# Decode attention beside an MLP on one core: the order of work behind the last K block, who copies the last P blocks, and matmuls per loop round

## The chip, the cores and the metric

One core of a Trainium2 chip. The metric is the device time of one execution in microseconds (us), the median of several runs. The engines are TensorE (PE; PEld is its weight load), VectorE (DVE), ScalarE (ACT) and GpSimd (POOL); SyncE (SP) issues nearly all transfers (DMA).

## What is computed

```python
W = min(4096, max(256, Sk // 4))                  # 2048 of the 8192 cached positions
q = (x @ wq).reshape(B, Sq, Hq, Dh)               # B=8, Sq=1, Hq=32, Dh=128, D=576
k = repeat(k_cache[:, :, Sk - W:, :], 2, axis=1)  # 16 heads of K and V, each for two heads of q
v = repeat(v_cache[:, :, Sk - W:, :], 2, axis=1)
p = softmax(einsum("bhqd,bhkd->bhqk", q, k) * Dh ** -0.5)
a = einsum("bhqk,bhkd->bhqd", p, v).reshape(B, Sq, Hq * Dh) @ wo
y = layernorm(x)
b = gelu(y @ w1 + b1) @ w2 + b2                   # F=4608
g = sigmoid((x * gate_w).sum(-1, keepdims=True))
return g * a + (1 - g) * b
```

All tensors are bf16. The window of K and of V is 67 MB each, against some 20 MB of weights; each byte is read once.

## The kernel before

The core reads 16 blocks of K and 16 of V, 4 MB each. Four groups (of 32 pairs of batch and K head) are each cut into four blocks of 512 positions, so block n belongs to group n // 4. Transfers are issued by SP in one order: wq, w1, K0, K1, V0, K2, V1, K3 and so on to K15, V14, V15, then b2, 24 rows of w2 in two pieces, wo in four pieces, and the last 12 rows of w2 in pieces of 8, 3 and 1 (here a row is one of the 36 rows that a partition holds). Four slots of on-chip memory take them in turn; the issue of a block waits until its slot is free. The slot of K15 takes the first three pieces of wo; the slot of V14 takes the fourth piece and the last three of w2.

For K block n (`k_unit`): VectorE makes four 32x32-block transposes (L693, `tr`), each into one of two halves of the tile `KT`; after each, TensorE adds one score unit (L711 and, through the helper that keeps the weights, L175), two groups of four matmuls of 512 columns. A transpose waits until the score unit of two transposes earlier has read its half. When all four units are done, `softmax` takes the maximum on VectorE (L644, `mx`), scales it (L646/L648, `nb`), and ScalarE makes the exponential P (L650); ScalarE then writes the mask for the next block's scores (L654).

For V block n (`v_item`): VectorE transposes P by 32x32 blocks (L668, `pt`, made in `spread`). Four block copies (L742 on ScalarE, L743 on GpSimd or VectorE) lay the result out as a block-diagonal operand; which engine takes each of the four is in `px_engs`. Then 64 matmuls multiply it with V (`pv`): two at the head, a hardware loop of rounds whose matmuls take their addresses from registers (L186, `BODY` of them in a round), two at the tail (L752). The last block, n = 15, has no loop: 48 and 16 matmuls (L752), its operand is laid out in the area of `KT`, which GpSimd first sets to zero (L726) when K15's scores are done. VectorE then adds the result to the running output (L788/L790, `o`). At a group's end come small sums across partitions (L674 to L681, with two tiny matmuls), a weighting on VectorE (L793, L796) and GpSimd (L798), and the matmul `us` (L801).

At the end, ScalarE and VectorE evict and transpose the attention output (L804, L805), and TensorE accumulates the product with wo (four blocks `proj0` to `proj3`, 16 matmuls each) and that with w2 (`m2`), all on L580, into one accumulator. Its order on TensorE: bias and the first 12 rows of w2 (28 matmuls), `us`, then 24 of the second 12 rows, 64 of the four blocks and 16 of the 8-row piece (104 together), four fillers into the score area, whose result nobody reads (`keep_warm`, L815 and L175), and 8 for the pieces of 3 and 1 rows. Two engines evict the accumulator (L885, L886) and two transfers write the output (L888).

The order on each engine is found when the program is built: a planner takes, of the operations that are ready, the one with the earliest start by the costs written beside them; `deps` are real waits, `after` only fixes an order of starts. So the costs decide the order, and nothing else at run time.

Of the kernel before, what the change touches and what calls it, by code (L numbers as in the profile page):

```python
# [38 lines left out]
class _Plan:  # L39
# [10 lines left out]
    def add(self, eng, fn, deps=(), name=None, cost=0.1, after=(), prio=0):  # L50
        op = _Op(eng, fn, deps, name, cost, after=after, prio=prio)
        op.idx = len(self.all)
        self.all.append(op)
        return op
# [138 lines left out]
def build_kernel(nc, A_x, A_k_cache, A_v_cache, A_wq, A_wo, B_x, B_w1, B_b1, B_w2, B_b2, gate_w, out):  # L193
# [10 lines left out]
    NL = 4 * NG  # L204
# [17 lines left out]
    with ExitStack() as es:  # L222
# [100 lines left out]
        maskq, maskv, swp, pair = view("maskq"), view("maskv"), view("swp"), view("pair")  # L323
# [45 lines left out]
        def col(i, parts=128):  # L369
# [3 lines left out]
        ps = es.enter_context(nc.psum_tensor("ps", [128, 8, 512], F32))  # L373
# [4 lines left out]
        BK_S = 6  # L378
# [8 lines left out]
        add, dma = P.add, P.dma  # L387
# [7 lines left out]
                   deps=[o_idf], name="r8", cost=0.2)  # L395
# [30 lines left out]
        for s in range(2):  # L426
            o_xz.append(add("dve", (lambda s=s: lambda e: e.tensor_copy(xz[:, s, :].rearrange("p (k z) -> p k z", z=2)[:, :, s], x_sb[:, 512:576]))(),  # L427
                            deps=dx + [o_xz0], name="xz%d" % s, cost=0.12))
# [12 lines left out]
        for s in range(2):  # L441
            o_yz.append(add("dve", (lambda s=s: lambda e: e.tensor_copy(yz[:, s, :].rearrange("p (k z) -> p k z", z=2)[:, :, s], y_bf[:, 512:576]))(),
                            deps=[o_y, o_yz0], name="yz%d" % s, cost=0.12))
# [35 lines left out]
        o_swp = []  # L479
# [108 lines left out]
        for vi in range(NL):  # L588
            stream.append(("V", vi))
            if vi + 2 < NL:  # L590
                stream.append(("K", vi + 2))
        HEAD, BODY, TAIL = 2, 20, 2
        ROUNDS = (64 - HEAD - TAIL) // BODY
        assert HEAD and TAIL and HEAD + ROUNDS * BODY + TAIL == 64
        held_regs = []
# [16 lines left out]
        grp_done, acc_done = {}, {}  # L612
        mask_done, mx_done = {}, {}
        grp_first, sums = {}, {}
        px_engs = [("pool", "pool", "act", "act")] * (NL - 1) + [("pool", "act", "act", "dve")]

        def take_slot():
            n = n_slot[0]
# [44 lines left out]
        def spread(n, after=()):  # L663
            g, i = divmod(n, 4)
            k = lambda m, j: sm[:, m, j:j + 1]
            MX, NB, S, AL, SS = range(5)
            ex, nb = ex_done[n], nb_done[n]
            pt_done[n] = add("dve", lambda e: e.transpose(bass.AP(arena, offset=aoffs("PT") + 2048 * (n % 2), ap=[[AST, 128], [1, 2048]]), Pm),  # L668
                             deps=[ex] + (px_done[n - 2] if n >= 2 else [o_yTp, o_hT]), name="pt%d" % n, cost=2.3, prio=5, after=after)
            if i == 3:  # L670
                G = lambda j: sg[:, g, j:j + 1]
                NBQ, WT, SW, RC, CF = range(5)
                prev = grp_done.get(g - 1, [])
                sw_pe = add("pe", lambda e: e.matmul(ps[:, BK_S, 4:5], swp, k(n, NB), start=True, stop=True), deps=[nb, o_u] + o_swp + prev, name="sw_pe%d" % g, cost=0.5, prio=3)  # L674
                nbq = add("dve", lambda e: e.tensor_tensor(out=G(NBQ), in0=k(n, NB), in1=ps[:, BK_S, 4:5], op=ALU.min), deps=[sw_pe], name="nbq%d" % g, cost=0.16, prio=3)
                grp_first[n] = nbq
                wt = add("act", lambda e: e.activation(out=G(WT), in_=k(n, NB), func=ACTF.Exp, bias=G(NBQ), scale=-1.0), deps=[nbq], name="wt%d" % g, cost=0.25, prio=3)
                sw = add("dve", lambda e: e.tensor_tensor(out=G(SW), in0=k(n, SS), in1=G(WT), op=ALU.mult), deps=[wt, ss_done[n]], name="sw%d" % g, cost=0.16, prio=3)
                su = add("pe", lambda e: e.matmul(ps[:, BK_S, 0:1], pair, G(SW), start=True, stop=True), deps=[sw, o_pair] + prev, name="sum_pe%d" % g, cost=0.5, prio=3)  # L679
                rc = add("dve", lambda e: e.reciprocal(out=G(RC), in_=ps[:, BK_S, 0:1]), deps=[su], name="rc%d" % g, cost=0.16, prio=3)  # L680
                cf = add("dve", lambda e: e.tensor_tensor(out=G(CF), in0=G(WT), in1=G(RC), op=ALU.mult), deps=[rc], name="cf%d" % g, cost=0.16, prio=3)  # L681
                grp_done[g] = [nbq, rc, cf]
                sums[g] = su

        def k_unit(n, s, d):
            g, i = divmod(n, 4)
            trs = []
            for rh in range(2):
                for hh in range(2):
                    m = 4 * n + 2 * rh + hh  # L690
                    kb = m % 2
                    deps = [d] + ([qk_half[m - 2]] if m >= 2 else [o_selp])
                    tr = add("dve", (lambda rh=rh, hh=hh, kb=kb: lambda e: e.transpose(bass.AP(arena_f, offset=foffs("KT") + kb * 2048, ap=[[AST // 2, 128], [1, 2048]]),  # L693
                                                                                      bass.AP(arena_f, offset=foffs("RAW") + s * SE + rh * (SE // 2) + 32 * hh, ap=[[AST // 2, 128], [64, 64], [1, 32]])))(),
                             deps=deps, name="tr%d_%d%d" % (n, rh, hh), cost=2.3, after=tr_hist[-1:] + ([mx_done.get(n - 1)] if rh + hh == 0 else []) + ([pt_done.get(n - 1)] if rh == 1 else []))
                    tr_hist.append(tr)
                    trs.append(tr)
                    if n and rh == 0 and hh == 1:
                        spread(n - 1, after=[tr])
                    if rh == 1 and hh == 0:  # L700
                        for op in (o_done.get(n - 2), grp_first.pop(n - 1, None)):
                            if op is not None:
                                op.after.append(tr)

                    def qk_fn(e, rh=rh, hh=hh, kb=kb):
                        mm = None
                        for ee in range(2):
                            for rc in range(4):
                                rhs = bass.AP(arena, offset=aoffs("KT") + kb * 4096 + rc * 1024 + ee, ap=[[AST, 128], [2, 512]])
                                args = (ps[:, rc, :], qbd[:, g % 2, 2 * hh + ee, rh, :], rhs)  # L710
                                mm = e.matmul(*args, start=False, stop=True, skip_group_check=True) if rc == 0 else held_matmul(nc, e, *args, stop=True, skip=True)  # L711
                        return mm
                    deps = [tr]
                    if rh == 0 and hh == 0:
                        deps += qb_done[g] + [mask_done[n]]
                    qk = add("pe", qk_fn, deps=deps, name="qk%d_%d%d" % (n, rh, hh), cost=1.85, after=qk_half[-1:] + pv_hist[-1:])
                    qk_half.append(qk)
            qk_unit[n] = qk
            if n > 4 and n % 4 == 1:
                us_done[(n - 5) // 4].after.append(qk)  # L720
            slot_free[s] = slot_free[s] + trs
            softmax(n)
            if n == NL - 1:
                o_kz.deps.append(qk)
# [3 lines left out]
        def v_item(n):  # L728
# [8 lines left out]
            for c in range(4):  # L737
                def fn(e, c=c):
                    dst = bass.AP(arena, offset=32 * c * AST + px_at + 32 * c, ap=[[AST, 32], [128, 64], [1, 32]])
                    src = bass.AP(arena, offset=32 * c * AST + aoffs("PT") + 2048 * (n % 2), ap=[[AST, 32], [32, 64], [1, 32]])  # L740
                    if px_engs[n][c] == "act":
                        return e.activation(out=dst, in_=src, func=ACTF.Copy)  # L742
                    return e.tensor_copy(dst, src)  # L743
                px_done[n].append(add(px_engs[n][c], fn, deps=[pt_done[n]] + px_free, name="qrx%d_%d" % (n, c), cost={"act": 1.8, "dve": 2.2, "pool": 4.0}[px_engs[n][c]], prio=5))

            def pv_part(a, b):
                def fn(e):
# [71 lines left out]
        def wo_all(_):  # L819
            def place(s, at, i):  # L820
                dst = slot(s)[:, at:at + WO_CH * D]
                h0 = WO_CH * i
                d = dma("sp", lambda e: e.dma_start(dst, A_wo[128 * h0:128 * (h0 + WO_CH), :].rearrange("(p j) c -> p (j c)", j=WOR)),
                        "o%d" % i, WO_CH * 128 * D * 2, deps=slot_free[s] if at == 0 else [], name="d_wo%d" % i, after=last_dma[-1:])
                last_dma.append(d)
                dj = dst.rearrange("p (j c) -> p j c", j=WOR)
                return AccGroup("proj%d" % i, [(oT[:, j, i, :], dj[:, j, :]) for j in range(WOR)], o_T + [d], cost=1.0, prio=1).op
            s = take_slot()
            done = [place(s, WO_CH * D * i, i) for i in range(3)]
            slot_free[s] = done  # L830
            s = take_slot()
            done = [place(s, 0, 3)]
            m2_at.append((s, WO_CH * D))
            slot_free[s] = done

# [8 lines left out]
        def m2_chunk(ci):  # L844
# [6 lines left out]
            for n, jn in enumerate(M_CUTS[ci]):  # L851
# [3 lines left out]
                mms = [(hT[:, j + k, 0:8], slot(s)[:, base + (at + k) * D:base + (at + k + 1) * D]) for k in range(jn)]  # L855
                ops.append(AccGroup("m2_%d_%d" % (ci, n), mms, [o_hT, d], cost=0.16 * jn, after=o_m2[-1:] + ([us_done[NG - 1]] if ci == 0 and n else [])).op)
                o_m2.append(ops[-1])
                if ci and n == 0:
                    o_m2.append(keep_warm("warm1", 4, [ops[-1]]))
                j, at = j + jn, at + jn  # L860
            slot_free[s] = slot_free[s] + ops

# [79 lines left out]
```

## Time and profile before

| | |
|---|---|
| time, median of 3 runs | 366.67 us (366.64 to 367.41) |
| the profiled execution | 366.57 us, span 365.3 us |
| bytes read | 154.31 MB, 422 GB/s over the span |
| busy share: PE, DVE, ACT, POOL | 77%, 68%, 37%, 22% |
| mean granted TensorE clock | 0.916 |

The profile is of one execution. Times in its rows are us from the span's start; the span ends with the last instruction, and the device time is a little longer. A row of the timeline gives start, duration, engine, source line, operation, output and input, count, and in brackets how long the engine was idle before and what released it. The end of a matmul is modelled, and a busy PE includes half-clock time. The granted clock is the share of full speed that TensorE was given.

### The profile page before, as it was taken

Reading aid. Unit: us, or ns where it says so; the run is one execution under the profiler, and the core shown is the slowest. Engines: PE = TensorE matmul, PEld = TensorE weight load, DVE = VectorE, ACT = ScalarE, POOL = GpSimd, SP = SyncE. Lnnn points to the kernel's source line nnn. Section 1 sums busy time; section 2 is a strip of 40 time slices with the busy share of each in tenths; the row PEclk is TensorE's granted clock in tenths of the full one; section 3 lists DMA queues with packets and bytes.
Section 4 is the critical chain, followed back from the end, with each engine's and each line's share of the span. In section 5 each row is a group of like instructions: output and inputs, shape, how many; then the busy total and the mean of one; then the engine's idle time right before and its main releaser. Section 6 shows DMA issues by size and latency. Waiting matters only on the chain.

```text
span 365.3 us, 4214 instructions
## 1 busy us (share of the span) xinstructions
PE 281.9 (77%) x1830; PEld 127.5 (35%) x1380; DVE 247.1 (68%) x191; ACT 135.4 (37%) x119; POOL 82.2 (22%) x79
## 2 busy tenths in 40 slices
PE   0455545999895979796969689796879698969597
PEld 0100000436170617060525234252517062605474
DVE  0723978797878695949495877677676959494320
ACT  1012106274544344444243324344444435442400
POOL 9123002130414040403121130304040404043200
PEclk9975696999999899899899989899989879989899
DMA  8999999999999999999999999999999999999994
GB/s 347 431 438 418 441 434 424 441 420 459 400 459 405 456 416 443 429 427 438 427 447 416 448 416 448 422 438 434 427 445 423 443 416 452 413 444 408 429 429 162
DMA packets 6580, 154.48 MB, mean 423 GB/s; under 512 B 764, under 2 KB 932, under 8 KB 1320
## 3 DMA queue, kind: packets, MB, share of 16 engines
q1 hardware_dynamic: 6512, 154.29, 98.2%
q8 instruction: 8, 0.13, 0.1%
q10 hardware_dynamic: 56, 0.03, 0.0%
q14 instruction: 4, 0.03, 0.0%
HBM read 154.31 MB, written 0.01 MB: 422 GB/s over the span
## 4 chain that ended last, share of the span: by engine, by line
DMA 45%; DVE 32%; PE 13%; issue 5%; ACT 3%; POOL 0%; ACTq 0%
DMA arena<-in_A_k_cache_dram 43%; DVE arena L693 18%; DVE arena L668 5%; PE ps L175 5%; DVE arena L644 3%; PE ps L752 2%; DMA arena<-in_gate_w_dram 2%; PE ps L580 2%; PE ps L711 1%; ACT arena L650 1%; PE ps L502 1%; ACT arena L742 1%; DVE arena L790 1%; DVE arena L563 1%; DVE arena L793 1%
## 5 line engine op out<-in xcount | busy, mean ns | idle before, releaser
L693 DVE STREAM_TRANSPOSE arena<-arena 128x2048 f32<-128x2048 f32 x64 | 145.2, 2287 | 27.7 <-DMA arena<-in_A_k_cache_dram 26.2
L175 PE MATMUL ps<-arena 128*128 128x512 bf16 (+2 forms) x450 | 130.3, 444 | 0.0
L743 POOL COPY arena<-arena 32x2048 bf16<-32x2048 bf16 x31 | 58.9, 1900 | 223.1 <-DVE arena L668 222.2
L186 PE MATMUL ps<-arena 128*128 x900 | 100.8, 273 | 0.0
L711 PE MATMUL ps<-arena 128*128 128x512 bf16 x128 | 54.6, 426 | 57.8 <-DVE arena L693 49.1
L186 PEld LDWEIGHTS ps<-arena 128*128 x900 | 88.1, 98 | 10.4
L742 ACT ACTIVATE arena<-arena 32x2048 bf16<-32x2048 bf16 x32 | 61.0, 1906 | 65.2 <-DVE arena L668 64.8
L650 ACT ACTIVATE arena<-ps,arena 128x2048 bf16<-128x2048 f32 x16 | 31.5, 1967 | 110.6 <-DVE arena L648 75.0
L711 PEld LDWEIGHTS ps<-arena 128*128 128x128 bf16 x128 | 13.3, 104 | 165.0 <-DVE arena L693 103.5
L644 DVE TENSOR_REDUCE arena<-ps 128x1 f32<-128x2048 f32 x16 | 36.7, 2292 | 38.1 <-PE ps L175 38.1
L668 DVE STREAM_TRANSPOSE arena<-arena 128x2048 bf16<-128x2048 bf16 x16 | 36.4, 2272 | 2.1 <-ACT arena L650 2.1
L654 ACT ACTIVATE ps<-arena 128x2048 f32<-128x2048 f32 x15 | 28.1, 1873 | 0.1
L752 PE MATMUL ps<-arena 128*128 128x256 bf16 x124 | 20.7, 294 | 4.0 <-ACT arena L742 4.0
L752 PEld LDWEIGHTS ps<-arena 128*128 128x128 bf16 x124 | 13.1, 107 | 19.3 <-issue 15.6
L453 PE MATMUL ps<-arena 8*128 8x8 bf16 x8 | 0.6, 171 | 14.5 <-DVE arena L427 9.4
L580 PE MATMUL ps<-arena 128*8 128x288 bf16 (+1 forms) x140 | 9.2, 286 | 0.0
L558 DVE TENSOR_TENSOR arena<-arena 128x1152 f32<-128x1152 f32 x1 | 1.4, 1359 | 11.1 <-ACT arena L556 11.1
L637 POOL COPY arena<-arena 32x128 bf16<-32x128 bf16 x16 | 4.6, 287 | 15.4 <-ACT arena L537 7.8
L580 PEld LDWEIGHTS ps<-arena 128*8 128x8 bf16 (+1 forms) x140 | 6.0, 86 | 3.7 <-issue 1.7
L680 DVE RECIPROCAL arena<-ps 128x1 f32<-128x1 f32 x4 | 0.6, 158 | 8.5 <-PE ps L679 8.5
L427 DVE COPY arena<-arena 8x64 bf16<-8x64 bf16 x2 | 0.3, 189 | 9.0 <-DMA arena<-in_gate_w_dram 9.0
L798 POOL TENSOR_TENSOR arena<-arena 128x256 f32<-128x256 f32 x4 | 2.4, 612 | 17.2 <-DVE arena L796 17.2
(105 smaller groups left out, 93.7 us busy)
## 6 DMA issues: line engine op xcount, KB each, us to landing
arena<-in_A_k_cache_dram SPq DMA_DIRECT2D x16, 4096.0 KB, 27.2
arena<-in_A_v_cache_dram SPq DMA_DIRECT2D x16, 4096.0 KB, 26.7
arena<-in_B_w_dram SPq DMA_DIRECT2D x1, 4608.0 KB, 23.1
arena<-in_A_wo_dram SPq DMA_DIRECT2D x4, 1152.0 KB, 20.4
arena<-in_A_wq_dram SPq DMA_DIRECT2D x1, 4096.0 KB, 12.7
arena<-in_B_w_dram SPq DMA_DIRECT2D x2, 1728.0 KB, 24.6
arena<-in_B_w_dram SPq DMA_DIRECT2D x1, 1152.0 KB, 20.0
arena<-in_B_w_dram SPq DMA_DIRECT2D x1, 576.0 KB, 24.1
```

The costliest lines, as they stand in the source:

```text
L175: return e.add_instruction(mybir.InstMatmult(name=nc.get_next_instruction_name(), engine=mybir.EngineType.PE, ins=[e.lower_ap(rhs), e.lowe ...
L186: return e.add_instruction(mybir.InstMatmult(name=nc.get_next_instruction_name(), engine=mybir.EngineType.PE, ins=[operand(r, r_ap), opera ...
L580: ins = e.matmul(ps[32 * j:32 * j + 8, BK_ACC, 0:JN], lhsT, rhs[:, JN * j:JN * j + JN], start=False, stop=True, skip_group_check=True, til ...
L644: mx = mx_done[n] = add("dve", lambda e: e.tensor_reduce(out=k(n, MX), in_=ps[:, 0:4, :].rearrange("p a n -> p (a n)"), axis=AXL.X, op=ALU ...
L650: ex = add("act", lambda e: e.activation(out=Pm, in_=ps[:, 0:4, :].rearrange("p a n -> p (a n)"), func=ACTF.Exp, bias=k(n, NB), scale=SCAL ...
L654: mask_done[n + 1] = add("act", lambda e: e.activation(out=ps[:, 0:4, :].rearrange("p a (n c) -> p (a n) c", c=32), in_=bass.AP(arena_f, o ...
L668: pt_done[n] = add("dve", lambda e: e.transpose(bass.AP(arena, offset=aoffs("PT") + 2048 * (n % 2), ap=[[AST, 128], [1, 2048]]), Pm), deps ...
L693: tr = add("dve", (lambda rh=rh, hh=hh, kb=kb: lambda e: e.transpose(bass.AP(arena_f, offset=foffs("KT") + kb * 2048, ap=[[AST // 2, 128], ...
L711: mm = e.matmul(*args, start=False, stop=True, skip_group_check=True) if rc == 0 else held_matmul(nc, e, *args, stop=True, skip=True)
L742: return e.activation(out=dst, in_=src, func=ACTF.Copy)
L743: return e.tensor_copy(dst, src)
L752: mm = e.matmul(ps[:, ob_, 0:256], lhsT, rhs, start=(k == 0), stop=True, skip_group_check=True)
```

## The change

Five edits. The four transposes of K15 follow each other on VectorE: P14's transpose (with o13 and what belongs to it) now comes after the fourth, where it came after the second. Of P14's four block copies GpSimd and ScalarE do one each and VectorE two (before: two and two); of P15's ScalarE does one and VectorE three (before: one on GpSimd, two on ScalarE, one on VectorE). GpSimd's zeroing for P15 is ordered after its copy of P14, and mx15 after VectorE's copies of P14. The four fillers behind the 8-row piece give way to five between `proj2` and `proj3` and five between `proj3` and the 8-row piece. The loop of `pv` has 12 matmuls in a round instead of 20, so five rounds instead of three. The planner's costs for block copies change too (VectorE 2.2 to 0.8, GpSimd 4.0 to 2.4); apart from the edits named, this moves only small things: in the groups 0 to 2, GpSimd's L798 comes behind its second block copy instead of between the two, and one small VectorE operation of group 0 (L678) comes one transpose later.

```diff
-        HEAD, BODY, TAIL = 2, 20, 2
+        HEAD, BODY, TAIL = 2, 12, 2
...
-        px_engs = [("pool", "pool", "act", "act")] * (NL - 1) + [("pool", "act", "act", "dve")]
+        px_engs = [("pool", "pool", "act", "act")] * (NL - 2) + [("pool", "act", "dve", "dve"), ("act", "dve", "dve", "dve")]
...
-                sw_pe = add("pe", lambda e: e.matmul(ps[:, BK_S, 4:5], swp, k(n, NB), start=True, stop=True), deps=[nb, o_u] + o_swp + prev, name="sw_pe%d" % g, cost=0.5, prio=3)
+                sw_pe = add("pe", lambda e: e.matmul(ps[:, BK_S, 4:5], swp, k(n, NB), start=True, stop=True), deps=[nb, o_u] + o_swp + prev, name="sw_pe%d" % g, cost=0.5, prio=3, after=pv_hist[-1:] if n == NL - 1 else [])
...
-                             deps=deps, name="tr%d_%d%d" % (n, rh, hh), cost=2.3, after=tr_hist[-1:] + ([mx_done.get(n - 1)] if rh + hh == 0 else []) + ([pt_done.get(n - 1)] if rh == 1 else []))
+                             deps=deps, name="tr%d_%d%d" % (n, rh, hh), cost=2.3, after=tr_hist[-1:] + ([mx_done.get(n - 1)] if rh + hh == 0 else []) + ([pt_done.get(n - 1)] if rh == 1 and n < NL - 1 else []))
...
-                    if n and rh == 0 and hh == 1:
+                    if n and (rh, hh) == ((1, 1) if n == NL - 1 else (0, 1)):
                         spread(n - 1, after=[tr])
-                    if rh == 1 and hh == 0:
+                    if (rh, hh) == ((1, 1) if n == NL - 1 else (1, 0)):
                         for op in (o_done.get(n - 2), grp_first.pop(n - 1, None)):
...
-                px_done[n].append(add(px_engs[n][c], fn, deps=[pt_done[n]] + px_free, name="qrx%d_%d" % (n, c), cost={"act": 1.8, "dve": 2.2, "pool": 4.0}[px_engs[n][c]], prio=5))
+                px_done[n].append(add(px_engs[n][c], fn, deps=[pt_done[n]] + px_free, name="qrx%d_%d" % (n, c), cost={"act": 1.8, "dve": 0.8, "pool": 2.4}[px_engs[n][c]], prio=5))
+
+            if n == NL - 2:
+                o_kz.after.append(px_done[n][0])
+                mx_done[n + 1].after.extend(op for op in px_done[n] if op.eng == "dve")
...
             done = [place(s, WO_CH * D * i, i) for i in range(3)]
+            warm = keep_warm("warm0", 5, done[2:])
             slot_free[s] = done
             s = take_slot()
             done = [place(s, 0, 3)]
+            done[0].after.append(warm)
+            o_m2.append(keep_warm("warm1", 5, done))
...
-                if ci and n == 0:
-                    o_m2.append(keep_warm("warm1", 4, [ops[-1]]))
```

## The prediction

> **What bounds the kernel now.** I read the page first: its chain of waits and its row of transfers.
>
> ```profile
> span 365.3 us, 4214 instructions
> DMA arena<-in_A_k_cache_dram 43%; DVE arena L693 18%; DVE arena L668 5%; PE ps L175 5%; DVE arena L644 3%; PE ps L752 2%; DMA arena<-in_gate_w_dram 2%; PE ps L580 2%; PE ps L711 1%; ACT arena L650 1%; PE ps L502 1%; ACT arena L742 1%; DVE arena L790 1%; DVE arena L563 1%; DVE arena L793 1%
> DMA  8999999999999999999999999999999999999994
> ```
>
> The transfers are busy from end to end, and 43% of the chain is waiting for K. Until the last K lands nothing but the volume of bytes counts; only after that can an order of work be worth anything. So I went on to the time after K15's landing: the timeline of VectorE, then that of the other engines (each row: start, duration, engine, line).
>
> ```profile
> 318.10 4.50 DVE L693 STREAM_TRANSPOSE arena<-arena 128x2048 f32<-128x2048 f32 x2 [3.35 <-DMA arena<-in_A_k_cache_dram]
> 322.53 2.27 DVE L668 STREAM_TRANSPOSE arena<-arena 128x2048 bf16<-128x2048 bf16 x1
> 324.72 2.27 DVE L693 STREAM_TRANSPOSE arena<-arena 128x2048 f32<-128x2048 f32 x1
> 326.91 0.44 DVE L790 SCALAR_TENSOR_TENSOR arena<-arena,ps 128x256 f32<-128x256 f32 x1
> 327.27 2.30 DVE L693 STREAM_TRANSPOSE arena<-arena 128x2048 f32<-128x2048 f32 x1
> 332.41 2.29 DVE L644 TENSOR_REDUCE arena<-ps 128x1 f32<-128x2048 f32 x1 [2.83 <-PE ps L175]
> 334.73 0.16 DVE L648 SCALAR_TENSOR_TENSOR arena<-arena 128x1 f32<-128x1 f32 x1
> 337.02 2.31 DVE L668 STREAM_TRANSPOSE arena<-arena 128x2048 bf16<-128x2048 bf16 x1 [2.13 <-ACT arena L650]
> 339.36 0.69 DVE L743 COPY arena<-arena 32x2048 bf16<-32x2048 bf16 x1
> ```
>
> Between the second and the fourth transpose of K15 stand P14's transpose (322.53) and o13 (326.91). The maximum mx15 (332.41) waits for the scores, P15's transpose for the exponential, and the block copies of P15 follow it at 339.36. What they release, and the end of the program, is on TensorE:
>
> ```profile
> 321.60 0.84 PE L175 MATMUL ps<-arena 128*128 128x512 bf16 x3
> ...
> 332.43 6.71 PE L186 MATMUL ps<-arena 128*128 x60
> ...
> 343.45 7.07 PE L752 MATMUL ps<-arena 128*128 128x256 bf16 x48 [3.98 <-ACT arena L742]
> ```
>
> ```profile
> 354.65 0.70 PE L801 MATMUL ps<-arena 128*128 128x256 f32 x2 [0.34 <-POOL arena L798]
> 355.28 6.54 PE L580 MATMUL ps<-arena 128*8 128x288 bf16 x104
> 361.75 0.39 PE L815 MATMUL ps<-arena 128*128 128x512 bf16 x1
> 361.97 0.81 PE L175 MATMUL ps<-arena 128*128 128x512 bf16 x3
> 362.71 0.66 PE L580 MATMUL ps<-arena 128*8 128x288 bf16 x8
> ```
>
> pv15's first 48 matmuls begin at 343.45, 3.98 us idle before them, released by ScalarE's second block copy. From 354.65 on TensorE never pauses: 104 matmuls, four fillers, the last eight, end at 362.71 + 0.66 = 363.37. Eviction and output take the rest of the span, 1.93 us. Did the last weights arrive in time? The issues on SP's queue, the time from issue to landing, and a window behind it (its last two numbers are DMA share and GB/s):
>
> ```profile
> 339.76 1.38 SPq L852 DMA_DIRECT2D arena<-in_B_w_dram  x3
> ```
>
> ```profile
> arena<-in_B_w_dram SPq DMA_DIRECT2D x1, 1152.0 KB, 20.0
> arena<-in_B_w_dram SPq DMA_DIRECT2D x1, 432.0 KB, 20.6
> arena<-in_B_w_dram SPq DMA_DIRECT2D x1, 144.0 KB, 20.5
> ```
>
> ```profile
> 361.00:362.00 1.00, 1.00 (x16) 0.46 (x10) 0.00 (x0) 0.00 (x0) 0.00 (x0) 1.00 0.00 0
> ```
>
> The three issues fill 1.38 us, about 0.46 apart, so the pieces of 8, 3 and 1 rows land at 339.76 + 20.0 = 359.8, 340.2 + 20.6 = 360.8 and 340.7 + 20.5 = 361.2; from 361 on nothing moves. The end is therefore set by the chain K15, scores, P15, pv15, projection, about 1.8 us behind a floor by the transfers: two matmuls after 361.2 could end at 361.2 + 0.05 + 0.35 = 361.6. So at most 363.37 - 361.6 = 1.8 us are to be had.
>
> **The change part by part.** *Four transposes together.* Two took 4.50 us, so four end at 318.10 + 9.0 = 327.1, where the fourth ended at 329.57. The third needs its KT half back from the first score unit; that ended at 321.60 + 0.84 = 322.44, before 322.6, so nothing waits. The last score unit, two groups of four matmuls of 512 columns, takes some 2.0 us (the four fillers from 361.75, of that width, took 0.96): to 329.1 instead of 332.4, and TensorE no longer pauses in front of it. o13 (0.44) and P14's transpose (2.27) now follow: 327.1 to 329.8. P14's copies start at 329.8, where they started at 324.8 before; the work that hid them was K15's scores, and that cover is now gone.
>
> *VectorE's copies of P14.* Before, GpSimd did two and ScalarE two; now one each, and VectorE two of 0.69 us. The price hangs on GpSimd:
>
> ```profile
> 324.86 3.83 POOL L743 COPY arena<-arena 32x2048 bf16<-32x2048 bf16 x2 [15.49 <-DVE arena L668]
> 332.43 3.51 POOL L726 MEMSET arena<- 128x4096 f32 x1 [3.75 <-PE ps L175]
> 339.39 2.40 POOL L743 COPY arena<-arena 32x2048 bf16<-32x2048 bf16 x1 [3.45 <-DVE arena L668]
> ```
>
> ```profile
> 32.60 3.51 POOL L606 MEMSET arena<- 128x4096 f32 x1 [5.24 <-PE ps L175]
> ...
> 35.14 1.59 DVE L559 TENSOR_SCALAR arena<-arena 128x1152 f32<-128x1152 f32 x1
> ```
>
> Beside VectorE's 0.69 us copy GpSimd's took 2.40 us and not 1.9: it ended as if it had begun when VectorE's was over. And a VectorE operation that started at 35.14 beside a GpSimd memset, which ended at 36.11, ended at 36.73. So each holds the other up. Bounds: if VectorE's two go back to back, they end at 329.85 + 1.4 = 331.25 and GpSimd's at 333.1; if GpSimd gets in between them, VectorE's second ends at 329.85 + 0.7 + 1.9 + 0.7 = 333.1. I take the second, as GpSimd is by then already waiting. The Trainium skill's page "SBUF — State Buffer", section "Who interferes with whom", says that the ports shared by the two engines go to whichever starts first, for a whole instruction, and that the other is blocked in full; 2.40 and 1.59 agree. By it a GpSimd memset that got in first would hold VectorE for its whole 3.5 us, and the sum would be 368.4 instead of 365.0.
>
> Either way pv14, which waits for all four copies, starts at about 333.2 (before: just ahead of its 60 loop matmuls at 332.43).
>
> *mx15 behind the copies.* From mx15's start to P15's copies were 339.36 - 332.41 = 6.95 us. From 333.1 that gives 340.05; VectorE's three copies, 2.1 us, end at 342.15 (by the lower bound 340.3). ScalarE's one ends sooner:
>
> ```profile
> 339.36 3.84 ACT L742 ACTIVATE arena<-arena 32x2048 bf16<-32x2048 bf16 x2 [1.77 <-DVE arena L668]
> ```
>
> It is two copies at 1.92. GpSimd has none left, and its memset of the old K area (3.51 us, after its own copy) is over by 336.7, before 340.
>
> *The clock.* TensorE now idles from 329.1 to 333.2. Windows of 3.41 us (first numbers: length, PE busy; third from the end: granted clock):
>
> ```profile
> 289.40:292.81 3.41, 2.49 (x7) 0.10 (x1) 2.41 (x2) 0.53 (x1) 2.49 (x2) 0.50 1.04 452
> 292.82:296.23 3.41, 3.41 (x10) 1.08 (x5) 0.72 (x1) 0.00 (x0) 0.00 (x0) 0.50 1.02 442
> 323.54:326.95 3.41, 1.09 (x5) 0.00 (x0) 3.41 (x3) 2.10 (x2) 2.04 (x2) 1.00 0.98 423
> 326.95:330.36 3.41, 3.31 (x8) 0.40 (x3) 2.62 (x3) 1.71 (x1) 1.73 (x1) 0.50 1.03 437
> ```
>
> A window busy for 1.09 of 3.41 us was followed by one at half the clock. pv14 will meet one: its 64 matmuls, 7.0 us at full clock (6.71 for 60), lose 3.41 / 2 = 1.7 us and end at 333.2 + 8.7 = 341.9. Bounds: no loss, 340.2; two such windows in a row, as at 289.40 and 292.82, the first begun in the idle time, some 3.0 lost, 343.2. With the two small matmuls behind it (0.3 us) and the copies at 342.15, pv15 starts at 342.25 (bounds 340.5 to 343.5), and now without a pause in front. Its 48 matmuls took 7.07 us; at pv14's rate, 7.0 / 64 = 0.109 each, they take 5.25 and end at 347.5 instead of 350.5. That is 3.0 us gained.
>
> *Fillers.* From 361.75 to 362.71 four fillers took 0.96 us, 0.24 each. Ten replace them: 2.4 us, 1.44 more on the way. They stand before the fourth block of the output matrix and before the 8-row piece; if TensorE waits for the transfers there, they cost nothing, otherwise all of it.
>
> *Rounds of twelve.* Five rounds of 12 replace three of 20 in 15 loops: 75 branches instead of 45.
>
> ```profile
> L186 PE MATMUL ps<-arena 128*128 x900 | 100.8, 273 | 0.0
> ```
>
> The 900 matmuls of the loops had no idle time before them, so a branch was hidden behind queued matmuls. Nothing, then; if one showed in full after all, it would be tenths of a microsecond in loops that wait for transfers anyway, and two more in pv14. Swapping two GpSimd operations in the earlier groups moves no consumer later.
>
> *Transfers.* The fourth block of the output matrix and the three pieces behind it wait for pv14's end, now 341.9 instead of some 339.4 (332.43 + 6.71 and the last two); as they needed some 20 us to land, they stand in a queue that this does not empty.
>
> *The sum.* Everything behind pv15 comes 3.0 us earlier: the 104 matmuls would end at 358.75, with ten fillers at 361.15, and the last eight at 361.8. The floor is 361.6. So 363.37 - 361.8 = 1.6 us less: span 363.7. The profiled execution took 366.57 us, 1.27 outside its span and 0.10 below the median of the runs, 366.67. Forecast: 366.57 - 1.6 = 365.0 us.
>
> **The rivals.** *The transfers' floor alone.* If the clock or the ports are kinder (pv15 at 340.5), the chain comes 4.8 us earlier, TensorE waits for the last piece, and the end is 361.6: 364.8 us. For it: the bounds above; against: the idle 4.1 us. In time it is the forecast, in the profile it shows as waits for transfers.
>
> *The clock stays at half.* pv14 loses 3.0 us, pv15 starts at 343.5, gains 1.8, and the fillers take 1.44 of that: end at 363.0, 366.2 us, no change that can be told. For it: the rows at 289.40 and 292.82, where 2.49 us of work at half clock did not bring the full one back. Against: the window from 326.95, as dense as pv14 will be (3.31 of 3.41), sufficed: the 60 matmuls from 332.43 ran at full clock. The Trainium skill's page "TensorE: Matmul & The Clock Gate", Part 1, says that the window runs freely and does not start with the kernel; by that, where the idle 4.1 us fall in it differs from run to run, and this rival could show in some runs only.
>
> *Slower: the memset cuts in.* GpSimd's memset is queued right behind its P14 copy. If GpSimd's copy comes first and the memset gets in between VectorE's two, VectorE waits 3.5 us more: mx15 at 336.6, P15's copies end at 345.6, pv15 runs from 345.7 to 350.95, later than before, and with the fillers the end is 363.37 + 0.45 + 1.44 = 365.2: 368.4 us. It decides as soon as pv15 starts after 343.85. For it: the operation at 35.14, held up by a memset. Against: at 339.36 VectorE's copy began 0.03 us before GpSimd's, and a VectorE copy that already waits should come before a memset that still waits for its own engine's copy.
>
> *The last pieces land 2.5 us later,* in step with their issue: end at 364.1, 367.3 us. Against it is the queue of some 20 us.
>
> **How the numbers follow.** Forecast with the floor, one result in time: 0.66. Clock: 0.13. Memset: 0.11. Late pieces: 0.04. Something unseen of either sign: 0.06. About 0.2%, 0.73 us, is what a measurement of this kernel can tell from no change. The clock's case lies between 365.0 and 366.2, half of it beyond that bound; of the unseen I count two thirds as faster, and half of the late pieces as slower: faster 0.66 + 0.065 + 0.04 = 0.76, slower 0.11 + 0.02 + 0.01 = 0.14, same the remaining 0.10. The range goes from a little below the floor, by the runs' own scatter, 364.4, to the clock's case, 366.3; the memset's and late pieces' cases stay outside.
>
> **What would show it.** Right: four transposes of K15 from 318.1 to 327.1; scores done near 329.1; VectorE's copies of P14 at 331.3 or 333.1; pv14 from 333.2, partly at half clock; pv15's 48 matmuls in 5.25 us without a pause in front; last piece at 361.2; last matmul at 361.6 to 361.8. Wrong: a VectorE copy of over 4 us (memset), pv15 starting after 343.85, gaps between the loops' rounds, or the last landing later than 361.5.

## The result and the profile after

| | before | changed |
|---|---|---|
| median, 14 runs each | 366.15 us (365.83 to 367.62) | 365.18 us (365.05 to 366.31) |
| ratio, 95% interval | | 0.997 (0.9959 to 0.9982) |
| the profiled execution | 366.57 us | 365.17 us |
| its span | 365.3 us | 363.9 us |

The changed kernel is faster, by 0.2% to 0.4%. The kernel before was run again beside each group of experiments; its medians there were 365.94 to 366.62 us, which is why each experiment is given with its ratio to that kernel, or beside the changed kernel's 365.18. The ratio is an estimate of its own, with a 95% interval, and not the quotient of the two medians, so the two can differ by some 0.1%. The VectorE timeline of the changed kernel behind K15's landing (start, duration, engine, line):

```profile
318.46 8.89 DVE L693 STREAM_TRANSPOSE arena<-arena 128x2048 f32<-128x2048 f32 x4 [3.52 <-DMA arena<-in_A_k_cache_dram]
327.28 0.44 DVE L794 SCALAR_TENSOR_TENSOR arena<-arena,ps 128x256 f32<-128x256 f32 x1
327.64 2.30 DVE L668 STREAM_TRANSPOSE arena<-arena 128x2048 bf16<-128x2048 bf16 x1
329.97 2.98 DVE L743 COPY arena<-arena 32x2048 bf16<-32x2048 bf16 x2
332.99 2.29 DVE L644 TENSOR_REDUCE arena<-ps 128x1 f32<-128x2048 f32 x1
335.31 0.16 DVE L648 SCALAR_TENSOR_TENSOR arena<-arena 128x1 f32<-128x1 f32 x1
337.60 2.31 DVE L668 STREAM_TRANSPOSE arena<-arena 128x2048 bf16<-128x2048 bf16 x1 [2.12 <-ACT arena L650]
339.94 2.12 DVE L743 COPY arena<-arena 32x2048 bf16<-32x2048 bf16 x3
```

Four transposes in a row, o13, P14's transpose, and mx15 no longer waits for TensorE: it stands right behind the two copies of P14. Those took 2.98 us, where twice 0.69 is 1.38: one by one, the first took 0.68 us and the second, from 330.69, 2.27. GpSimd's timeline says why:

```profile
330.00 2.40 POOL L743 COPY arena<-arena 32x2048 bf16<-32x2048 bf16 x1 [20.62 <-DVE arena L668]
332.52 3.88 POOL L726 MEMSET arena<- 128x4096 f32 x1
```

GpSimd's copy ended at 332.40 as if it had begun 0.5 us late, and VectorE's second copy at 332.95, 0.55 us behind that, somewhat less than the length of a copy. The memset, which started while that second copy was still under way, then ran 0.37 us over its usual 3.51. What followed on TensorE, and its clock in windows of 3.41 us (length, PE busy; third from the end the granted clock):

```profile
333.50 8.28 PE L186 MATMUL ps<-arena 128*128 x60
341.62 0.38 PE L756 MATMUL ps<-arena 128*128 128x256 bf16 x2
341.84 0.28 PE L674 MATMUL ps<-arena 128*128 128x1 f32 x2
342.21 5.40 PE L756 MATMUL ps<-arena 128*128 128x256 bf16 x48
```

```profile
329.91:333.32 3.41, 0.22 (x2) 0.13 (x2) 3.31 (x4) 1.91 (x1) 3.20 (x2) 1.00 0.91 394
333.32:336.73 3.41, 3.41 (x18) 2.32 (x17) 2.12 (x2) 1.22 (x1) 3.09 (x1) 0.50 0.96 404
336.73:340.14 3.41, 3.41 (x33) 3.06 (x32) 2.51 (x2) 1.60 (x5) 0.00 (x0) 1.00 1.00 426
```

The loop of pv14 took 8.28 us instead of 6.71: one window at half clock behind an idle one. pv15 starts at 342.21 without a pause, and its 48 matmuls take 5.40 us instead of 7.07. The end of TensorE's timeline, and the last landings:

```profile
351.74 0.70 PE L805 MATMUL ps<-arena 128*128 128x256 f32 x2 [0.35 <-POOL arena L802]
352.37 4.58 PE L580 MATMUL ps<-arena 128*8 128x288 bf16 x72
357.11 1.03 PE L175 MATMUL ps<-arena 128*128 128x512 bf16 x4 [0.16 <-issue]
358.06 1.15 PE L580 MATMUL ps<-arena 128*8 128x288 bf16 x16
359.14 0.39 PE L819 MATMUL ps<-arena 128*128 128x512 bf16 x1
359.37 1.03 PE L175 MATMUL ps<-arena 128*128 128x512 bf16 x4
360.33 1.64 PE L580 MATMUL ps<-arena 128*8 128x288 bf16 x24
```

```profile
342.40 1.38 SPq L859 DMA_DIRECT2D arena<-in_B_w_dram  x3
```

```profile
arena<-in_B_w_dram SPq DMA_DIRECT2D x1, 1152.0 KB, 17.4
arena<-in_B_w_dram SPq DMA_DIRECT2D x1, 432.0 KB, 18.0
arena<-in_B_w_dram SPq DMA_DIRECT2D x1, 144.0 KB, 17.8
```

(Of the first five fillers this trace lacks the record of the first matmul, so 0.16 us of TensorE's time there looks idle.) The last pieces were issued 2.6 us later than before and landed at the same time, 342.40 + 17.4 = 359.8 and 343.3 + 17.8 = 361.1: the queue ahead of them was long enough. (343.3 is the start of the third issue; the three start about 0.46 apart.) The last matmul ended at 360.33 + 1.64 = 361.97, 1.40 earlier than before. No matmul here waited for a transfer: the 8-row piece lay ready at 359.8 while TensorE was at its second five fillers.

### The profile page after: what moved, and what is told of

It is laid out like the page before. It is cut to its first block, busy times and chain, and to the rows that moved or that the text cites. A ratio compares the mean times of both kernels' runs of the same rounds, so it can differ in the third digit from the quotient of the medians.

```text
span 363.9 us, 4246 instructions
## 1 busy us (share of the span) xinstructions
PE 277.4 (76%) x1818; PEld 126.9 (35%) x1381; DVE 254.9 (70%) x195; ACT 131.6 (36%) x117; POOL 78.8 (22%) x77
## 4 chain that ended last, share of the span: by engine, by line
DMA 45%; DVE 35%; PE 13%; issue 4%; ACT 2%; POOL 0%; ACTq 0%
DMA arena<-in_A_k_cache_dram 43%; DVE arena L693 20%; DVE arena L668 5%; PE ps L175 4%; PE ps L186 2%; PE ps L756 2%; DMA arena<-in_gate_w_dram 2%; PE ps L580 2%; DVE arena L644 2%; DVE arena L797 1%; PE ps L502 1%; DVE arena L794 1%; DVE arena L743 1%; PE ps L711 1%; DVE arena L563 1%
## 5 line engine op out<-in xcount | busy, mean ns | idle before, releaser
L175 PE MATMUL ps<-arena 128*128 128x512 bf16 (+2 forms) x446 | 126.8, 432 | 11.6 <-DVE arena L693 8.3
L743 POOL COPY arena<-arena 32x2048 bf16<-32x2048 bf16 x29 | 55.1, 1902 | 227.1 <-DVE arena L668 212.2
L186 PE MATMUL ps<-arena 128*128 x900 | 102.3, 275 | 0.0
L711 PE MATMUL ps<-arena 128*128 128x512 bf16 x121 | 50.5, 417 | 50.1 <-DVE arena L693 43.4
L742 ACT ACTIVATE arena<-arena 32x2048 bf16<-32x2048 bf16 x30 | 57.2, 1906 | 70.5 <-DVE arena L668 67.8
L711 PEld LDWEIGHTS ps<-arena 128*128 128x128 bf16 x128 | 13.2, 103 | 162.5 <-DVE arena L693 104.7
L756 PE MATMUL ps<-arena 128*128 128x256 bf16 x124 | 19.0, 275 | 3.8 <-DVE arena L743 3.7
L756 PEld LDWEIGHTS ps<-arena 128*128 128x128 bf16 x124 | 12.0, 99 | 17.0 <-issue 14.0
L794 DVE SCALAR_TENSOR_TENSOR arena<-arena,ps 128x256 f32<-128x256 f32 x12 | 5.4, 447 | 1.4 <-PE ps L756 1.4
## 6 DMA issues: line engine op xcount, KB each, us to landing
arena<-in_B_w_dram SPq DMA_DIRECT2D x1, 1152.0 KB, 17.4
```

The source lines that it names most:

```text
L175: return e.add_instruction(mybir.InstMatmult(name=nc.get_next_instruction_name(), engine=mybir.EngineType.PE, ins=[e.lower_ap(rhs), e.lowe ...
L186: return e.add_instruction(mybir.InstMatmult(name=nc.get_next_instruction_name(), engine=mybir.EngineType.PE, ins=[operand(r, r_ap), opera ...
L756: mm = e.matmul(ps[:, ob_, 0:256], lhsT, rhs, start=(k == 0), stop=True, skip_group_check=True)
```

## The experiments

**What sets the end.** The first asks whether the fillers are on the way. The changed kernel without them:

```diff
-            warm = keep_warm("warm0", 5, done[2:])
...
-            done[0].after.append(warm)
-            o_m2.append(keep_warm("warm1", 5, done))
```

> The changed kernel without its ten fillers. Theory (ten fillers lie on the way to the end by 0.4 us, since the last piece lands at 361.2 and the last matmul ended at 362.0): TensorE waits for the pieces, the last matmul ends at 361.6, 364.75 us, 0.4 less than the changed kernel's 365.18. Rival (the fillers keep the clock up while TensorE waits for the last pieces): a half-clock window over the last 40 matmuls, 366 us or more.

Measured: 364.74 us (364.63 to 364.78), ratio to the kernel before 0.9955 (0.994 to 0.9971). The end of its TensorE timeline:

```profile
352.40 5.79 PE L580 MATMUL ps<-arena 128*8 128x288 bf16 x88
359.81 1.72 PE L580 MATMUL ps<-arena 128*8 128x288 bf16 x24 [1.63 <-DMA arena<-in_B_w_dram]
```

Now the last 24 matmuls wait 1.63 us for the 8-row piece and end at 361.53, with the landings. So the ten fillers cost 0.44 us. The clock didn't fall without them: the granted clock was 1.00 from 356.8 to the end, and the 24 matmuls took 1.72 us, against 1.64 with the fillers.

The changed kernel with the four fillers in their old place, behind the 8-row piece:

```diff
-            warm = keep_warm("warm0", 5, done[2:])
...
-            done[0].after.append(warm)
-            o_m2.append(keep_warm("warm1", 5, done))
...
+                if ci and n == 0:
+                    o_m2.append(keep_warm("warm1", 4, [ops[-1]]))
```

> The changed kernel with the four fillers where they stood before, behind the 8-row piece. Theory (what is left to gain is set by the landings; 0.96 us of fillers behind the 8-row piece's landing at 359.8 can't be hidden): 8-row piece's matmuls end at 360.85, fillers at 361.8, last matmul 362.4, 365.6 us, 0.4 over the changed kernel. Rival (place and number of fillers don't matter, only the chain to pv15): the same as the changed kernel, 365.2.

Measured: 365.73 us (365.52 to 365.84), ratio 0.9976 (0.9964 to 0.9988). TensorE:

```profile
359.82 1.15 PE L580 MATMUL ps<-arena 128*8 128x288 bf16 x16 [1.63 <-DMA arena<-in_B_w_dram]
360.90 0.39 PE L819 MATMUL ps<-arena 128*128 128x512 bf16 x1
361.13 0.81 PE L175 MATMUL ps<-arena 128*128 128x512 bf16 x3
361.87 0.66 PE L580 MATMUL ps<-arena 128*8 128x288 bf16 x8
```

The wait is there again, and behind it four fillers that delay pieces which have landed. 365.73 - 364.74 = 0.99 us is their 0.97 us (360.90 to 361.87). As long as the fillers stand there and the 8-row piece lands at 359.8, an earlier pv15 doesn't bring the end below 362.5.

Ten fillers at each of the two places of the changed kernel instead of five:

```diff
-            warm = keep_warm("warm0", 5, done[2:])
+            warm = keep_warm("warm0", 10, done[2:])
...
-            o_m2.append(keep_warm("warm1", 5, done))
+            o_m2.append(keep_warm("warm1", 10, done))
```

> The changed kernel with ten fillers at each of the two places instead of five. Theory (TensorE waits for nothing behind pv15 in the changed kernel, so more fillers are paid in full at 0.235 each): 2.35 us more, 367.5. Rival (the fillers stand in waits for the pieces of weights and are hidden): within 0.3 us of 365.18.

Measured: 367.39 us (367.11 to 368.18), ratio 1.0022 (1.0006 to 1.0039), 2.2 over the changed kernel, where 2.35 was expected: paid almost in full.

The kernel before without its fillers, all else as it was:

```diff
-                if ci and n == 0:
-                    o_m2.append(keep_warm("warm1", 4, [ops[-1]]))
```

> The kernel before without its four fillers and nothing else. Theory (they stood on the way to the end for their whole 0.96 us): 0.96 less than the kernel before of the same call, down to the floor of 364.75 where its chain is early. Rival (they keep the clock up for the last eight matmuls): no faster than the kernel before.

Measured: 365.25 us (364.8 to 366.54) against 365.94 for the kernel before in that call, ratio 0.9968 (0.9952 to 0.9985). The medians differ by 0.69 us; the interval holds the 0.96 us (0.9974) that the theory gives and excludes the rival. So taking four fillers away and nothing else gains about what the whole change gained. The profile doesn't show the wait for the landing: the profiled execution took 366.35 us, its pv15 met half clock (7.82 us for the 48 matmuls), and no matmul waits at its end.

**The parts alone.** The kernel before with the four transposes together; GpSimd's zeroing is ordered behind its copies of P14:

```diff
-... ([pt_done.get(n - 1)] if rh == 1 else []))
+... ([pt_done.get(n - 1)] if rh == 1 and n < NL - 1 else []))
-                    if n and rh == 0 and hh == 1:
+                    if n and (rh, hh) == ((1, 1) if n == NL - 1 else (0, 1)):
...
+            if n == NL - 2:
+                o_kz.after.append(px_done[n][1])
```

> The kernel before with the four transposes of K15 together, its old block copies (GpSimd's zeroing behind its copies of P14), old fillers, rounds of 20. Theory: scores done near 329.2, P14's copies 329.9 to 333.7, pv14 from 333.8 at partly half clock to 342.5, pv15 from 342.85 without a pause, 2.4 us earlier than before; but the fillers behind the 8-row piece's landing hold the end at 362.4: 365.6 us. Rival (the copies on VectorE bring the gain; transposes alone only move the waiting behind the zeroing): pv15 not before 343.4 and the time as before, 366.2.

Measured: 365.65 us (365.54 to 365.95), ratio 0.9984 (0.9975 to 0.9993), the time as expected, the way only in part: pv15 began at 343.75 and not 342.85. K15 landed 0.6 us later than in the profile of before, and pv14 met two half-clock windows in a row, the first begun in the idle time before it: the granted clock was 0.78 in the window from 330.36, 0.50 in that from 333.77 and 0.72 in that from 337.18, and its loop took 8.85 us. It didn't matter to the end, since the 8-row piece came later still: TensorE waited 0.58 us for it. Its VectorE and GpSimd timelines show one more hold-up, taken up in the last section:

```profile
332.40 1.70 DVE L648 SCALAR_TENSOR_TENSOR arena<-arena 128x1 f32<-128x1 f32 x1
```

```profile
330.25 3.83 POOL L743 COPY arena<-arena 32x2048 bf16<-32x2048 bf16 x2 [20.93 <-DVE arena L668]
```

nb15, one number per partition, took 1.70 us instead of 0.16 and ended at 334.10, with GpSimd's second copy (334.08).

The kernel before with P15's copies alone on ScalarE and VectorE:

```diff
-... * (NL - 1) + [("pool", "act", "act", "dve")]
+... * (NL - 1) + [("act", "dve", "dve", "dve")]
```

> The kernel before with P15's copies alone on ScalarE (one) and VectorE (three), nothing else. Theory (each way of getting pv15 forward ends at the same landing plus the old fillers): copies done 2.1 us after P15's transpose instead of 3.85, pv15 starts some 1.8 us earlier; the 8-row piece's matmuls wait for the landing, the old fillers and the last eight follow: the end is where the transposes alone brought it, 365.65 us. Rival (gains of the parts add up, the copies are half of the change): between 365.2 and 365.4.

Measured: 365.73 us (365.54 to 367.27), ratio 0.9981 (0.9963 to 0.9998). The end on TensorE:

```profile
359.80 1.15 PE L580 MATMUL ps<-arena 128*8 128x288 bf16 x16 [1.02 <-DMA arena<-in_B_w_dram]
361.85 0.66 PE L580 MATMUL ps<-arena 128*8 128x288 bf16 x8
```

It ends at 362.51. With either part alone the end stands where the old fillers put it; the gains don't add up.

The kernel before with rounds of twelve:

```diff
-        HEAD, BODY, TAIL = 2, 20, 2
+        HEAD, BODY, TAIL = 2, 12, 2
```

> The kernel before with rounds of 12 and nothing else. Theory (a round's branch is hidden behind queued matmuls, and the loops wait for transfers): the same as the kernel before, within 0.2 us, and no idle time before the loops' matmuls. Rival (each branch shows as some tenths of a us and reaches the end through pv14): 0.3 us or more slower.

Measured: 366.05 us against 366.6, ratio 0.9998 (0.9986 to 1.001). The groups of the loops' matmuls, on its page:

```profile
L186 PE MATMUL ps<-arena 128*128 x900 | 100.7, 273 | 0.0
```

No idle time, and 100.7 us busy against 100.8: the rounds change nothing that these runs can tell.

**GpSimd beside VectorE's copies.** The changed kernel with the zeroing ahead of GpSimd's copy of P14:

```diff
-                o_kz.after.append(px_done[n][0])
+                px_done[n][0].after.append(o_kz)
```

> The changed kernel with GpSimd's zeroing ordered ahead of its copy of P14 instead of behind. Theory (a GpSimd memset that runs holds VectorE's copies up until it ends): memset 329.2 to 332.7, VectorE's copies of P14 begin only then, mx15 starts between 334.1 and 336.0 instead of 333.0, and the time rises by as much, 366.3 to 368.2 us. Rival (a memset only writes and does not hold VectorE's copies up): VectorE's copies end at 331.4, mx15 starts 1.6 us earlier; pv14 waits for GpSimd's copy until 334.6 and ends at 343.3 at partly half clock, pv15 starts 1.4 us later, 366.5.

Measured: 368.0 us (367.87 to 369.06), ratio 1.005 (1.0028 to 1.0072), near the later end of the theory's window. The timeline of all engines but TensorE from the memset on:

```profile
329.44 3.51 POOL L726 MEMSET arena<- 128x4096 f32 x1 [20.17 <-PE ps L175]
329.96 1.91 ACT L742 ACTIVATE arena<-arena 32x2048 bf16<-32x2048 bf16 x1 [10.96 <-DVE arena L668]
329.96 5.82 DVE L743 COPY arena<-arena 32x2048 bf16<-32x2048 bf16 x2
333.08 2.15 POOL L743 COPY arena<-arena 32x2048 bf16<-32x2048 bf16 x1
```

VectorE's two copies of 0.69 us took 5.82, one by one 3.53 and 2.27: the first waited for the memset's end (332.95), the second for the end of GpSimd's copy (335.23). The rival said 1.4 us for the two and falls. This comes close to the slower rival of the prediction, 368.0 where it said 368.4, but in another order: here the memset is ahead of both of VectorE's copies, there it comes between them.

The changed kernel with no copy of P14 on GpSimd:

```diff
-... [("pool", "act", "dve", "dve"), ("act", "dve", "dve", "dve")]
+... [("act", "dve", "dve", "dve"), ("act", "dve", "dve", "dve")]
```

> The changed kernel with no copy of P14 on GpSimd: ScalarE one, VectorE three. Theory (GpSimd's copy held VectorE's second one up for some 1.6 us): VectorE's three end 2.1 us after the first began, mx15 starts at 332.1 instead of 333.0, pv15 at 341.3 instead of 342.2; all ten fillers then fit before the landings and the end is the floor, 364.75. Rival (no hold-up, 0.69 us a copy was never the price of two): three copies take longer than the two did, 3 us or more, and the time is 365.2 or above.

Measured: 368.45 us (367.84 to 369.4), ratio 1.0053 (1.0034 to 1.0073). The theory was not tested, and the rival, whose numbers (over 3 us, over 365.2) came about, did not come about for its reason: the edit did more than was meant. The order that kept the memset back hung on P14's first copy, now on ScalarE, and an `after` between two engines is no wait:

```profile
329.46 3.51 POOL L726 MEMSET arena<- 128x4096 f32 x1 [20.05 <-PE ps L175]
329.98 4.96 DVE L743 COPY arena<-arena 32x2048 bf16<-32x2048 bf16 x3
```

The memset started before VectorE's three copies, and these ended at 334.94, 2.0 us behind the memset's end (332.97). The planner had also put o14 (pv14's result added to the running output), which waits for pv14, ahead of P15's third copy. The same without fillers:

```diff
-... [("pool", "act", "dve", "dve"), ("act", "dve", "dve", "dve")]
+... [("act", "dve", "dve", "dve"), ("act", "dve", "dve", "dve")]
...
-            warm = keep_warm("warm0", 5, done[2:])
...
-            done[0].after.append(warm)
-            o_m2.append(keep_warm("warm1", 5, done))
```

> The changed kernel without fillers and without GpSimd's copy of P14. Theory (the last landing is the floor): pv15 0.9 us earlier than in the changed kernel, and the same time as without the fillers alone, 364.75 us, with a longer wait of TensorE for the 8-row piece. Rival (the chain still counts): some 0.9 us less, 363.9.

Measured: 366.32 us (365.42 to 366.96), ratio 0.9995 (0.9979 to 1.001). With the same fault in it (pv15 began at 345.04, and no matmul waited at the end), it could not test the floor.

So once more, with the zeroing waiting for VectorE's copies of P14 and o14 behind P15's copies:

```diff
-... [("pool", "act", "dve", "dve"), ("act", "dve", "dve", "dve")]
+... [("act", "dve", "dve", "dve"), ("act", "dve", "dve", "dve")]
...
-                o_kz.after.append(px_done[n][0])
+                o_kz.deps.extend(op for op in px_done[n] if op.eng == "dve")
+
+            if n == NL - 1:
+                o_done[n - 1].after.extend(op for op in px_done[n] if op.eng == "dve")
```

> The changed kernel, ten fillers included, with no copy of P14 on GpSimd, its zeroing waiting for VectorE's copies of P14, and o14 behind P15's copies on VectorE. Theory (what held VectorE up in the changed kernel was GpSimd, copy or memset): three copies of P14 in 2.1 us, mx15 at 332.1, pv15 at 341.3, 0.9 earlier; the ten fillers then end by the landings and the end is the floor, 364.75. Rival (VectorE's copies are slow in a row by themselves): 3 us or more for the three, and 365.2 or above.

Measured: 364.88 us (364.71 to 365.25), ratio 0.9969 (0.9957 to 0.9981). VectorE, and the end on TensorE:

```profile
330.14 2.12 DVE L743 COPY arena<-arena 32x2048 bf16<-32x2048 bf16 x3
```

```profile
359.95 1.72 PE L580 MATMUL ps<-arena 128*8 128x288 bf16 x24 [0.26 <-DMA arena<-in_B_w_dram]
```

Three copies in 2.12 us, sooner than the two beside GpSimd (2.98); and with ten fillers still in it, TensorE now waits 0.26 us for the 8-row piece. The fillers have become free to within some 0.1 us, because the chain is earlier.

**A version of two edits.** P15's copies as in the change and no fillers, all else as before:

```diff
-... * (NL - 1) + [("pool", "act", "act", "dve")]
+... * (NL - 1) + [("act", "dve", "dve", "dve")]
...
-                if ci and n == 0:
-                    o_m2.append(keep_warm("warm1", 4, [ops[-1]]))
```

> The kernel before with two small edits: P15's copies on ScalarE (one) and VectorE (three), and no fillers. Theory (the landing is the floor, and these two suffice to reach it): TensorE waits for the 8-row piece, the last matmul ends some 0.35 us behind the last landing, 364.75 us, 0.4 below the changed kernel. Rival (the other edits are needed for the last part): 365.2 or above.

Measured: 364.79 us (364.63 to 364.85), ratio 0.9963 (0.995 to 0.9977). The end on TensorE:

```profile
359.92 1.73 PE L580 MATMUL ps<-arena 128*8 128x288 bf16 x24 [1.63 <-DMA arena<-in_B_w_dram]
```

With 364.74 for the change without fillers these are the fastest of the study, and both end with the last landing. Here pv15 began at 341.58, in the change without fillers at 342.24, and the last matmul ended at 361.65 and 361.53: 0.66 us less of chain brought nothing more, which is what a floor by the landings says. For this time, then, the transposes together, VectorE's copies of P14, the rounds and the new fillers are not needed; with the floor reached, the end no longer shows what each is worth.

## Why the prediction was right, and where it was off

It said 365.0 us, faster; measured were 365.18, within the range. By its own steps:

- *Four transposes together*: from landing to the end of the fourth 8.9 us (predicted 9.0), and mx15 no longer behind TensorE. Right.
- *VectorE's copies of P14*: the upper of the two bounds was taken, GpSimd in between, 3.25 us for the two; it was 2.98, in that order. Right, and the experiments bear the mechanism out: 2.12 us for three copies without GpSimd, 5.82 us for two behind a memset.
- *The clock*: one half-clock window in pv14, 8.7 us predicted for its 64 matmuls, and 8.74 measured from the start of the first (333.10) to the start of what follows (341.84). pv15 at 342.21 (predicted 342.25), without a pause and at full clock. That this fits to 0.04 us is partly luck: K15 landed 0.36 us later than in the profile that the sum was worked out from (318.46 against 318.10), and the transposes and VectorE's copies of P14 took together some 0.5 us less than forecast.
- *Fillers*: predicted at 0.24 us each, all of it on the chain, with the end 0.2 us behind the floor at 361.6. The end was 361.97 against the predicted 361.8, and without the fillers, at the floor, 361.53. Of the 0.17 us between 361.97 and 361.8, 0.09 had come up by the matmul `us` (pv15's 48 matmuls took 5.40 us and not 5.25), the rest behind it. What the prediction had the wrong way round is the worth of this edit: it stands there as a price of 1.44 us, but the old four behind the 8-row piece would have held the end at 362.5, where the runs that keep them and wait for that piece have it (362.51 and 362.53, and 362.75 where it landed later). With them in the changed kernel it takes 365.73 us, so the new place gained 0.55 us, though there are ten now instead of four.
- *Rounds of twelve* and *transfers*: nothing, and the landings as before, as predicted.

*What was off* is the size of the gain: 1.6 us forecast, 0.97 between the medians (1.40 between the two profiled executions). The term that was mis-sized is mainly the time it was subtracted from: 0.42 of the 0.63 us lie between 366.57 and the median 366.15, the rest is the later end described above. In the profiled execution of before, the third score unit fell into a half-clock window (the row at 326.95) and mx15 began at 332.41. In the profiled execution of the kernel with rounds of twelve, same order of work, 365.92 us, it did not:

```profile
331.67 2.29 DVE L644 TENSOR_REDUCE arena<-ps 128x1 f32<-128x2048 f32 x1 [2.07 <-PE ps L175]
```

That is 0.74 us earlier. Since nothing behind the chain was waiting, this went through to the end: 365.92 against 366.57. The prediction, with three runs at hand, took 366.57 for the kernel's time, where 14 runs had the median 366.15. The Trainium skill's page "TensorE: Matmul & The Clock Gate", Part 1, says that the window runs freely and the kernel's start does not set it; two executions of the same order of work, one with a half-clock window there (mx15 at 332.41) and one without (331.67), agree with that. That it accounts for the whole scatter of the kernel before was not tried.

*The rivals.* The floor was reached only when the fillers were gone or the chain earlier; then 364.74 to 364.88, the 364.8 of that rival. The clock's rival was not seen in the profile; three of the 14 runs took 365.9 to 366.3, which would fit it, but they were not profiled, and their mean granted clocks (0.934, 0.939 and 0.925) are about those of the other eleven (0.930 to 0.939), so what made them longer stays open. The memset's did not occur: GpSimd's memset stood right behind its copy, as that rival has it, but VectorE's second copy, which was already waiting, went first (it ended at 332.95, and the memset took 3.88 us instead of 3.51). That is what the prediction held against this rival; with the memset ahead, in the other order of the experiment, the price was near the one stated. The rival of the late pieces did not occur: they were issued later by 2.6 us and landed at the same time.

## What to carry to other kernels

When the last transfer lands shortly before the end, work out the floor that it sets first; what an edit to the chain can gain ends there. Filler work behind a landing that the engine waits for is paid in full (0.99 us for four here); ahead of that landing it is free only as far as it fits into the wait (ten were free to some 0.1 us with the early chain, and cost 0.44 us in the changed kernel). Before a copy moves from GpSimd to VectorE, look at what GpSimd runs beside it, memsets too, and keep that away with a wait, as an `after` between two engines is none. And take the time to subtract from out of several runs, above all where the profile shows half-clock windows next to short pauses.

## What the runs showed of the hardware

Not expected: that the smallest of VectorE's operations can be held up by a GpSimd copy. With the transposes alone, nb15, which has two inputs, took 1.70 us beside such a copy and ended with it, while beside a memset it took 0.16 us (at 334.73 in the kernel before). It was seen in one execution. The Trainium skill's page "SBUF — State Buffer", section "Who interferes with whom", has this case: a VectorE instruction with two inputs from SBUF contends with a GpSimd instruction that reads SBUF, not with one that only writes it; both rows agree. And a memset on GpSimd does hold VectorE's block copies up, which have one input: the one that started at 329.96 beside a memset took 3.53 us instead of 0.69 and ended 0.54 us behind the memset. It doesn't hold everything up: mx15, whose input are the scores, took 2.29 us beside the memset in both kernels (at 332.41 and 332.99).
